# Moving the experts' first-weight loads to SyncE's queue, weighting the batch sums on VectorE, halving the maxima across engines and copying gate rows less often

## The chip, the core and the metric

The kernel runs on one core of a Trainium2 chip. The core has TensorE (PE in the profile, its weight loads PEld), VectorE (DVE), ScalarE (ACT), GpSimd (POOL) and SyncE (SP). They run on their own and wait for one another by semaphores. Work is done on tiles in SBUF (128 partitions); TensorE writes to PSUM. SP, ACT and POOL can issue transfers (DMAs). The metric is the device time in microseconds (us) of one execution: the median of three runs before the change is 1496.69 us (1496.05 to 1498.59).

## What is computed

```python
def _attn_ref(x, filt_r, filt_i):            # x 8 x 3072 x 256
    X = np.fft.rfft(x, axis=1)
    Y = X * (filt_r + 1j * filt_i)[None, :, :]
    return np.fft.irfft(Y, n=x.shape[1], axis=1)

def _moe_ref(x, phi, w1, w2):                # x 24576 x 256, 8 experts of 4 slots
    logits = x @ phi                         # 24576 x 32
    d = exp(logits - logits.max(0));  d /= d.sum(0) + 1e-9
    slot_input = d.T @ x                     # 32 x 256, over all eight batches
    for e in range(E):
        h = np.maximum(slot_input[e] @ w1[e], 0.0)
        slot_out[e] = h @ w2[e]
    c = exp(logits - logits.max(1));  c /= c.sum(1) + 1e-9
    return c @ slot_out

def _moe2_ref(x, w_gate, w_val, w_out):
    g = x @ w_gate
    return (g * sigmoid(g) * (x @ w_val)) @ w_out
```

Output: 24576 x 256, float32.

## The kernel before

The kernel has three parts, one after the other: `phase1`, `transition`, `phase2`.

**Phase 1** transforms the eight batches. A step is one half (128 columns) of a batch, 16 steps with 6 units each; the loop `for i, (s, u) in enumerate(units)` writes out by hand, unit by unit, what each engine does, and every engine works in that order. A unit multiplies by the DFT (`s2_unit`, line 258), multiplies with the filter on VectorE (lines 262 and 263, tiles P and Q), adds on POOL, and two units later transposes on TensorE (`tr_unit`, line 283, one PSUM buffer T) with an evacuation on ScalarE (line 284, tile y). Beside it run generators that the loop steps on:

- `chain(b)`, one for each batch: the logits (tile lg in SBUF, copied from PSUM by ScalarE at line 400), the maximum of each slot (VectorE, line 398, over both PSUM halves at once, then a transpose at line 411 and a second maximum at line 412 into mb), the exponentials (lines 423, 429, 434), a transform of them (lines 447 to 474), and the product with the transformed batch (line 482), which gives the batch's sum for the slots. The sums of batches 0 to 5 go out to memory and come back into `slots` (`kept`); batch 6 is copied there (line 496).
- `conv`: a rounding of w_gate, w_val and w_out on ScalarE, VectorE and POOL, in the pool `cvp` (8 KB in each partition).
- `first_weights`: the combine weights c of batch 0.

In the last two steps the experts' first weights are loaded (`load_w1`, line 134, 512 KB each): thirteen issues from ScalarE's queue, three from SyncE's after the loop (expert 6 and half of 7). Behind the loop the end of chain 6 (`g6`) and chain 7 (`g7`) are taken in turns: `for g in (g6, g7, g6, g7, g7, g6, g7, g6, g6)`. `combine` forms each batch's weight from the maxima (`al`, `beta4`), spreads it over a diagonal `rb`, and 14 small products (line 548) add seven batches' weighted sums; line 502 adds the eighth. That is `slot_input`.

**Transition**: `load_w2` (line 765, 1 MB each, from SP's queue in the order 6, 7, 0, gate weights, 5, 4, 1, 2, 3, value weights), the experts' first product (`stage1`, line 807), second product (`stage2`, line 832, first with experts 0 to 3), and with its result the small gate and value matrices for phase 2 (`g4`, `v4`). These hold in 128 rows four copies of 32: a rounded part (hi) and the rest (lo). The first third is split on VectorE (line 872); the two others are made as `gh` and `gl` (lines 886, 887) and copied by 16 DMAs (line 890), 8 from SP and 8 from POOL.

**Phase 2** runs 576 items of 512 tokens x 128 columns: gate and value products (lines 983, 984), SiLU on ScalarE (line 986, tile s), product and split on VectorE and ScalarE (h, hi, lo: lines 992, 999, 1000), and LAG items later the projection into four PSUM tiles (lines 1011 and 1015). `load_out(f)` splits the output weights wo (ScalarE line 972, POOL line 973) for items 0 to 11. Every twelfth item the four tiles are evacuated (lines 1024, 1025) and written out (line 1028).

SBUF is handed out in pools as stacks from the left and from the right. The tiles of the transition lie in a row from the left: w2_0 (8 KB), hs (8), w2_1 to w2_3 (24), ht (8), so and sot (2), gh (2), gl (2), a pad (10), and on. Phase 2's pool `kp` is opened when they have been given back, from the left again: s 3 x 2, h 3 x 2, hi 5 x 2, lo 5 x 2, tmp 4 x 1, ot 2 x 4 KB, 44 KB in all. A pool that takes over memory waits with its first instruction on each engine until everything that used that memory is done.

Of the kernel before, what the change touches and what calls it, by code (L numbers as in the profile page):

```python
# [22 lines left out]
EXP_AT = 17  # L23
HOLD = 9
# [55 lines left out]
def spectral_softmoe_glu_kernel(  # L80
# [56 lines left out]
    def phase1():  # L137
        with ExitStack() as c1:
# [4 lines left out]
            cvp = c1.enter_context(tc.tile_pool(name="cvp", bufs=1))  # L143
# [164 lines left out]
            def chain(b, last):  # L308
# [78 lines left out]
                cm = chp.tile([128, E], F32, tag="cm", name="cm")  # L387
# [9 lines left out]
                both = bass.AP(pl[0].tensor, pl[0].offset, [list(pl[0].ap[0]), [16, E], [512, 2], [1, 16]])  # L397
                dve.tensor_reduce(out=cm, in_=both, axis=AX.XY, op=ALU.max)
                for h in range(2):
                    act.copy(lg[h], pl[h].rearrange("p (e n) -> p e n", n=16))  # L400
# [11 lines left out]
                dve.tensor_reduce(  # L412
                    out=mb[:, b:b + 1],
                    in_=ps[0:32, 0:128].rearrange("p (g n) -> p g n", g=2)[:, :, 0:48],
# [30 lines left out]
                for h in range(2):  # L445
                    for g in range(2):
                        pe.matmul(
                            out=pl[64 * h:64 * h + 64, g],
                            lhsT=s1t_sb[64 * g:64 * g + 48, :],
                            rhs=dd[64 * g:64 * g + 48, h],  # L450
                            tile_position=(64 * g, 64 * h),
                        )
                for es in es2:
                    turn(bd, pl[:, :, es].rearrange("p g e n -> p e g n"), es)
                yield
                ps = two(True)
                for jj in range(NJ):
                    g, k = jj % 4, jj // 4
                    pe.matmul(
                        out=col(ps, k)[32 * g:32 * g + 32],  # L460
                        lhsT=bd[:, :, jj],
                        rhs=fwd[:, jj, :],
                        tile_position=(0, 32 * g),
                    )
                dt_ = evac("dt", ps)
# [7 lines left out]
                for k in range(6):  # L473
                    pe.transpose(out=col(ps, k), in_=col(dt_, k), identity=ident)
                if last:
                    rb, pss = next(com)
                dh = evac("dh", ps)
                yield
                ps = two(True)[0] if b == NB - 2 else small()
                for k in range(6):  # L480
                    for g in range(4):
                        pe.matmul(  # L482
                            out=ps[32 * g:32 * g + 32, 0:D],
                            lhsT=col(dh, 4 * k + g, 32),
                            rhs=yt[b, k][:, g, :],
                            start=(k == 0),
                            stop=(k == 5),
                            tile_position=(0, 32 * g),
                        )
                    if k in (2, 5) and b == NB - 2:  # L490
                        yield
# [4 lines left out]
                act.copy(sl, ps[:, 0:256])  # L496
                if b < NB - 2:
                    nc.scalar.dma_start(out=sld[:, b, :], in_=sl)
                if last:
                    next(com)  # L500
                    for d_ in range(2):
                        pe.matmul(
                            out=pss[d_][:, 0:32], lhsT=sl[:, d_ * 128:(d_ + 1) * 128], rhs=rb[:, b, :],
                            start=False, stop=True,
                        )
                        (dve.tensor_copy if d_ else act.copy)(sp[:, d_, :], pss[d_][:, 0:32])
# [10 lines left out]
            def combine():  # L517
# [5 lines left out]
                beta4 = chp.tile([128, NB, 1], F32, tag="beta4", name="beta4")  # L523
                dve.tensor_reduce(out=mx, in_=mb, axis=AX.X, op=ALU.max)
                dve.tensor_scalar(al, mb, mx, None, ALU.subtract)
                act.activation(al, al, AF.Exp)
                yield
# [4 lines left out]
                dve.tensor_scalar(al, al, sm, 2.0 / SEQ, ALU.mult, ALU.mult)  # L532
                yield
                rb = chp.tile([128, NB, 32], F32, tag="t4", name="rb")
                psb = ps_t.tile([128, 512], F32, tag="T", name="psb")
                pe.matmul(out=psb[:, 0:NB], lhsT=rep4[0:32, :], rhs=al)
                dve.tensor_copy(beta4[:, :, 0], psb[:, 0:NB])
                dve.tensor_tensor(
                    out=rb,
                    in0=rep4[:, None, 0:32].to_broadcast([128, NB, 32]),  # L540
                    in1=beta4.to_broadcast([128, NB, 32]),
                    op=ALU.mult,
                )
                pss = [ps_x.tile([128, 512], F32, tag="X", name="pss") for _ in range(2)]
                yield rb, pss
                for d_ in range(2):
                    for b in range(NB - 1):
                        pe.matmul(
                            out=pss[d_][:, 0:32],
                            lhsT=slots[b // 4][:, b % 4, d_ * 128:(d_ + 1) * 128],  # L550
                            rhs=rb[:, b, :],
                            start=(b == 0),
                            stop=False,
                        )
                yield

# [90 lines left out]
            xp += [cr.enter_context(tc.tile_pool(name=f"xp{k}", bufs=1, side="right")) for k in (1, 0)][::-1]  # L647
            load_x(0, 0)
# [52 lines left out]
            for i, (s, u) in enumerate(units):  # L701
# [16 lines left out]
                if (s, u) in ((2 * NB - 2, 0), (2 * NB - 1, 0)):  # L718
                    wt = xp[s % 2].tile([128, 2, 2, FE], F32, tag="x", name="w")
                    for k in range(2):  # L720
                        load_w1(nc.scalar, 2 * (s % 2) + k, enumerate(wt[:, k, t] for t in range(2)))
                if (s, u) == (2 * NB - 1, 0):
                    load_w1(nc.scalar, 4, [(t, sgp.tile([128, FE], F32, tag="sg", name="w")) for t in range(2)])
                if (s, u) == (2 * NB - 1, 1):
                    wt = bp[0].tile([128, 3, FE], F32, tag="b", name="w")
                    load_w1(nc.scalar, 5, ((0, wt[:, 0]), (1, wt[:, 1])))
                    load_w1(nc.scalar, 7, ((0, wt[:, 2]),))
# [10 lines left out]
            load_w1(nc.sync, 6, ((0, wt[:, 0]), (1, wt[:, 1])))  # L738
            load_w1(nc.sync, 7, ((1, wt[:, 2]),))
# [7 lines left out]
            for g in (g6, g7, g6, g7, g7, g6, g7, g6, g6):  # L747
                next(g, None)
# [7 lines left out]
    def transition():  # L756
# [13 lines left out]
        w2s[0] = one([128, 8, D], "w2_0")  # L770

# [9 lines left out]
        one([128, 10 * D], "pad")  # L781
# [82 lines left out]
        for w, dst in gates:  # L864
# [6 lines left out]
            for r in (32, 96):  # L871
                dve.tensor_tensor(out=dst[r:r + 32, :], in0=pg[r:r + 32], in1=dst[r:r + 32, :], op=ALU.subtract)
# [25 lines left out]
    def phase2_tiles():  # L898
# [7 lines left out]
        def first():  # L906
            t = cp.tile([128, 3, 2, 512], F32R, tag="c4", name="c4", bufs=2)

            for r in range(4):
                (nc.sync if r < 2 else nc.scalar).dma_start(  # L910
                    out=t[32 * r:32 * r + 32].rearrange("p q G n -> p q (G n)").bitcast(F32),
                    in_=cd[r // 2].rearrange("q e n -> e q n"),
                )
            c4[0] = t
            for c in range(3):
# [3 lines left out]
                )  # L919

        def build(b):
# [31 lines left out]
            for q in range(3):  # L953
                for r in range(4):
                    nc.sync.dma_start(
                        out=t[32 * r:32 * r + 32, q].rearrange("p G n -> p (G n)").bitcast(F32),
                        in_=(ch if r < 2 else cl)[32 * q:32 * q + 32, :].bitcast(F32),
# [4 lines left out]
        return {"cp": cp, "g4": g4, "v4": v4, "wo": wo, "c4": c4, "build": build, "first": first}  # L962

    def phase2(later):
        cp, g4, v4, wo, c4, build = (later[k] for k in ("cp", "g4", "v4", "wo", "c4", "build"))
# [3 lines left out]

        def load_out(f):  # L970
            st = wo[f][:, 1, :].bitcast(F32)
            act.copy(wo[f][:, 0, :], st)
            pool.tensor_tensor(out=wo[f][:, 1, :], in0=st, in1=wo[f][:, 0, :], op=ALU.subtract)  # L973
# [28 lines left out]

        def proj(i):
            b, q, G, f = items[i]
            hi, lo = hhi.pop(i), hlo.pop(i)
            if f == 0:
                acc[0] = [ps_o.tile([128, 512], F32, tag=f"o{t}", name=f"o{t}") for t in range(4)]
            for t in range(4):
                a = acc[0][t]
                ts = slice(128 * t, 128 * t + 128)  # L1010
                pe.matmul(  # L1011
                    out=a, lhsT=hi[:, ts], rhs=wo[f].rearrange("p k d -> p (k d)"),
                    start=(f == 0), stop=(f == NF - 1), skip_group_check=True,
                )
                pe.matmul(  # L1015
                    out=a[:, D:2 * D], lhsT=lo[:, ts], rhs=wo[f][:, 0, :],
                    start=False, stop=(f == NF - 1), skip_group_check=True,
                )
            if f == NF - 1:
                ot = kp.tile([128, 4, D], F32, tag="ot", name="ot", bufs=2)  # L1020
                for t in range(4):
                    a = acc[0][t]
                    tmp = kp.tile([128, D], F32, tag="tmp", name="tmp", bufs=4)
                    act.copy(tmp, a[:, D:2 * D])  # L1024
                    dve.tensor_tensor(out=ot[:, t, :], in0=a[:, 0:D], in1=tmp, op=ALU.add)  # L1025
# [14 lines left out]
        todo = list(range(len(items)))  # L1040
        gen = build(1)
        for i in range(len(items) + LAG):
# [11 lines left out]
            if i < NF:  # L1054
                load_out(i)
            if 0 <= i - 1 < len(items):
                split(i - 1)
            if i % 4 == 1 and i > NF:
                next(gen, None)

# [36 lines left out]
```

## Time and profile before

| | |
|---|---|
| median of three runs | 1496.69 us |
| the profiled execution: its own time, its span | 1495.89 us, 1494.1 us |
| phase 1 with its end, until the experts' first product | 0 to 379.7 us |
| transition, until the first gate product | 379.7 to 405.9 us |
| phase 2 | 405.9 to 1494.1 us |
| TensorE busy, share of the span | 96% |
| VectorE, ScalarE | 78%, 64% |

The profile is one execution. Its times count from the span's start; "idle" stands in brackets behind an instruction with what ended it. PEclk is the share of TensorE's full clock that was granted. Instructions that issue DMAs are shown on queues of their own (SPq, ACTq).

### The profile page before, as it was taken

What the parts mean: (1) busy time and instruction counts of PE and PEld (TensorE: products, weight loads), DVE (VectorE), ACT (ScalarE), POOL (GpSimd) and SP (SyncE); (2) the same over time, 40 slices, a digit from 0 to 9 for tenths busy, and PEclk for the clock granted to TensorE, in tenths of its full rate; (3) what the DMA queues carried; (4) which work ended last, traced back from release to release, by engine and by line L of the source; (5) the groups of instructions that cost most, each with busy time, mean ns of one, the idle gap of its engine ahead of it and who ended that gap; (6) DMA issues with size and microseconds to landing.
All of it is one profiled execution on the core that took longest, in us unless ns stands there. A gap on an engine that the chain in (4) does not pass through costs nothing.

```text
span 1494.1 us, 25173 instructions
## 1 busy us (share of the span) xinstructions
PE 1441.1 (96%) x9574; PEld 1152.9 (77%) x9574; DVE 1158.3 (78%) x1870; ACT 960.8 (64%) x1838; POOL 243.1 (16%) x315
## 2 busy tenths in 40 slices
PE   4899999998999999999999999999999999999998
PEld 2566566665488888888888888888888888888887
DVE  2788888876278878878887887888789778877775
ACT  1476666653267667666766766676676667666665
POOL 0466666653020000000000000000000000000000
PEclk9999999999999999999999999999999999999999
DMA  9978888859710220120031012112110211211011
GB/s 225 159 122 156 155 145 149 156 151 364 254 39 16 52 58 17 44 64 18 25 71 29 25 36 55 34 29 49 47 29 22 65 39 24 48 43 26 19 29 29
DMA packets 87848, 116.42 MB, mean 78 GB/s; under 512 B 8880, under 2 KB 65072, under 8 KB 87600
## 3 DMA queue, kind: packets, MB, share of 16 engines
q1 hardware_dynamic: 80480, 102.37, 31.4%
q10 hardware_dynamic: 6800, 11.54, 2.6%
q8 instruction: 75, 1.23, 0.4%
q0 software_dynamic: 448, 0.92, 0.2%
q14 instruction: 45, 0.37, 0.1%
HBM read 68.13 MB, written 34.60 MB: 69 GB/s over the span
## 4 chain that ended last, share of the span: by engine, by line
PE 84%; DVE 7%; DMA 3%; ACT 2%; issue 2%; POOL 1%; ACTq 0%; SPq 0%; DVEq 0%; POOLq 0%
PE o L1011 35%; PE o L1015 18%; PE V L984 9%; PE G L983 9%; PE X L258 3%; PE s L230 2%; PE T L283 2%; DVE sg L238 2%; DVE Q L263 1%; PE c L482 1%; DMA fraw<-in_filt_i_dram 1%; DVE P L262 1%; PE L L291 1%; DMA nyq<-in_filt_r_dram 1%; DMA lgf<-lgd 1%
## 5 line engine op out<-in xcount | busy, mean ns | idle before, releaser
L1011 PE MATMUL o<-wo,hi 128*128 128x512 f32 x2304 | 833.4, 396 | 2.7 <-POOL wo L973 2.7
L1015 PE MATMUL o<-wo,lo 128*128 128x256 f32 x2304 | 645.5, 280 | 0.0
L986 ACT ACTIVATE s<-G 128x512 f32<-128x512 f32 x576 | 344.7, 598 | 323.1 <-PE G L983 320.1
L992 DVE TENSOR_TENSOR h<-V,s 128x512 f32<-128x512 f32 x576 | 395.0, 686 | 172.0 <-ACT s L986 171.2
L1011 PEld LDWEIGHTS o<-wo,hi 128*128 128x128 f32 x2304 | 433.1, 188 | 106.8 <-POOL wo L973 3.0
L1015 PEld LDWEIGHTS o<-wo,lo 128*128 128x128 f32 x2304 | 434.8, 189 | 25.3
L1000 DVE TENSOR_TENSOR lo<-h,hi 128x512 fp32r<-128x512 f32 x576 | 422.4, 733 | 1.1
L999 ACT CAST hi<-h 128x512 fp32r<-128x512 f32 x576 | 354.6, 616 | 11.7 <-DVE h L992 8.3
L984 PE MATMUL V<-c,v 128*128 128x512 f32 x576 | 227.7, 395 | 1.1 <-DVE h L992 1.1
L983 PE MATMUL G<-c,g 128*128 128x512 f32 x576 | 228.3, 396 | 0.2 <-ACT s L986 0.2
L258 PEld LDWEIGHTS X<-fwd,b 128*128 128x128 f32 x768 | 94.3, 193 | 58.5 <-issue 40.0
L983 PEld LDWEIGHTS G<-c,g 128*128 128x128 f32 x576 | 108.3, 188 | 26.2 <-ACT s L986 0.9
L238 DVE STREAM_TRANSPOSE sg<-s 128x1024 f32<-128x1024 f32 x64 | 79.3, 1241 | 60.0 <-PE s L230 57.7
L258 PE MATMUL X<-fwd,b 128*128 128x128 f32 x768 | 110.6, 288 | 3.3 <-ACT b L247 1.8
L984 PEld LDWEIGHTS V<-c,v 128*128 128x128 f32 x576 | 108.8, 189 | 3.1 <-DVE h L992 2.4
L930 POOL TENSOR_TENSOR lg<-lg,mx 96x1024 f32<-96x1024 f32 x7 | 16.9, 2409 | 565.8 <-DVE mx L928 565.8
L1025 DVE TENSOR_TENSOR ot<-o,tmp 128x256 f32<-128x256 f32 x192 | 70.1, 423 | 39.6 <-ACT tmp L1024 39.6
L247 ACT COPY b<-sg 128x768 f32<-128x768 f32 x64 | 58.9, 923 | 64.6 <-DVE sg L238 64.5
L230 PE MATMUL s<-x,csm 48*64 48x512 f32 x512 | 73.4, 636 | 20.0 <-DMA x<-in_x_dram 17.5
L271 POOL TENSOR_TENSOR yt<-P 128x256 f32<-128x256 f32 x96 | 70.3, 732 | 115.9 <-DVE P L262 115.1
L262 DVE TENSOR_TENSOR P<-X,ft 128x512 f32<-128x512 f32 x96 | 64.1, 668 | 12.2 <-PE X L258 11.3
L273 POOL TENSOR_TENSOR yt<-Q 128x256 f32<-128x256 f32 x95 | 71.1, 748 | 0.2
(197 smaller groups left out, 979.9 us busy)
## 6 DMA issues: line engine op xcount, KB each, us to landing
out_dram<-ot SPq DMA_DIRECT2D x192, 128.0 KB, 2.2
x<-in_x_dram SPq DMA_DIRECT2D x60, 384.0 KB, 8.2
w<-in_moe_w_dram SPq DMA_DIRECT2D x8, 1024.0 KB, 11.4
w<-in_moe_w_dram ACTq DMA_DIRECT2D x13, 512.0 KB, 7.8
c<-ch SPq DMA_DIRECT2D x42, 128.0 KB, 2.4
c<-cl SPq DMA_DIRECT2D x42, 128.0 KB, 2.4
raw<-in_moe_w_gate_dram SPq DMA_DIRECT2D x12, 256.0 KB, 5.8
raw<-in_moe_w_val_dram SPq DMA_DIRECT2D x12, 256.0 KB, 5.2
```

Of the source, the lines that this page charges most:

```text
L230: pe.matmul(out=ps[64 * k:64 * k + 64, 16 * r:16 * r + 16, :], lhsT=s1t_sb[64 * r:64 * r + 48, :], rhs=xt[step][64 * r:64 * r + 48, k, :, ...
L238: dve.transpose(out=sg.rearrange("p j d k -> p d j k"), in_=ps.rearrange("p n d -> p d n"))
L258: pe.matmul(out=ps[:, g].rearrange("p r m -> p (r m)"), lhsT=bb[:, j, :], rhs=fwd[:, j, :])
L262: dve.tensor_tensor(out=P, in0=ps, in1=f, op=ALU.mult)
L983: pe.matmul(out=pg, lhsT=g4[c][:, fs], rhs=c4[b][:, q, G, :])
L984: pe.matmul(out=pv, lhsT=v4[c][:, fs], rhs=c4[b][:, q, G, :])
L986: act.activation(s, pg, AF.Silu)
L992: dve.tensor_tensor(out=h, in0=pv, in1=s, op=ALU.mult)
L999: act.copy(hi, h)
L1000: dve.tensor_tensor(out=lo, in0=h, in1=hi, op=ALU.subtract)
L1011: pe.matmul(out=a, lhsT=hi[:, ts], rhs=wo[f].rearrange("p k d -> p (k d)"), start=(f == 0), stop=(f == NF - 1), skip_group_check=True,)
L1015: pe.matmul(out=a[:, D:2 * D], lhsT=lo[:, ts], rhs=wo[f][:, 0, :], start=False, stop=(f == NF - 1), skip_group_check=True,)
```

## The change

- The maxima: VectorE takes the maximum of one PSUM half while ScalarE's copy is written for the other, and then the other way round; the two columns of maxima are transposed by two products.
- The batch sums: `combine` adds the weighted sums on VectorE in seven steps (`add`), placed between steps of chain 7, and the eighth as the evacuation of the product; the 14 products of line 548 go. Chain 6's last product is cut into four pieces, and the pieces stand between the steps of chain 7.
- The loads: all first weights go out from SP's queue. `cvp` is on the right now, is given back at the last step's first unit, and expert 6's weights take its place. w2_0 leaves the left end of the row and stands behind gl; it is loaded last but one.
- The gates: rows are ordered hi, hi, lo, lo, so that one subtraction does for two; three `load_out` steps (EARLY) are moved ahead of the copies. Of the 16 copies 12 are issued by SP and 4 by POOL.
- The last two items are projected tile by tile (`part`, `evac`, `close`), and each pair of tiles is written out when it is done, from three queues.

```diff
+EARLY = 3
...
-            cvp = c1.enter_context(tc.tile_pool(name="cvp", bufs=1))
+            cvs = ExitStack()
...
+                plv = [t.rearrange("p (e n) -> p e n", n=16) for t in pl]
                 for h in range(2):
-                    act.copy(lg[h], pl[h].rearrange("p (e n) -> p e n", n=16))
+                    dve.tensor_reduce(out=cm[:, h], in_=plv[1 - h], axis=AX.X, op=ALU.max)
+                    act.copy(lg[h], plv[h])
...
-                pe.transpose(out=ps[0:32, 0:128], in_=cm, identity=ident)
+                for h in range(2):
+                    pe.transpose(out=ps[0:32, 128 * h:128 * h + 128], in_=cm[:, h], identity=ident)
...
-                    if k in (2, 5) and b == NB - 2:
+                    if k >= 2 and b == NB - 2:
                         yield
...
-                act.copy(sl, ps[:, 0:256])
+                if last:
+                    rb, beta4, acc = next(com)
+                    dve.scalar_tensor_tensor(sl, ps[:, 0:256], beta4[:, b:b + 1], acc, ALU.mult, ALU.add)
+                else:
+                    act.copy(sl, ps[:, 0:256])
...
+                def add(b):
+                    row = slots[b // 4][:, b % 4, :]
+                    if b == 0:
+                        dve.tensor_scalar(row, row, beta4[:, 0:1], None, ALU.mult)
+                    else:
+                        acc = slots[0][:, 0, :]
+                        dve.scalar_tensor_tensor(acc, row, beta4[:, b:b + 1], acc, ALU.mult, ALU.add)
+
+                for b in range(3):
+                    add(b)
                 yield
...
-                for d_ in range(2):
-                    for b in range(NB - 1):
-                        pe.matmul(
...
+            cvp = cvs.enter_context(tc.tile_pool(name="cvp", bufs=1, side="right"))
...
-                        load_w1(nc.scalar, 2 * (s % 2) + k, enumerate(wt[:, k, t] for t in range(2)))
+                        load_w1(nc.sync, 2 * (s % 2) + k, enumerate(wt[:, k, t] for t in range(2)))
...
+                if (s, u) == (2 * NB - 1, 0):
+                    for _ in side:
+                        pass
+                    cvs.close()
+                    w6 = cr.enter_context(tc.tile_pool(name="w6", bufs=1, side="right"))
+                    load_w1(nc.sync, 6, enumerate(w6.tile([128, FE], F32, tag=f"w{t}", name="w") for t in range(2)))
...
-            for g in (g6, g7, g6, g7, g7, g6, g7, g6, g6):
+            for g in (g6, g7, g6, g7, g7, g6, g7, g6, g7, g6, g7, g6, g6):
...
-        w2s[0] = one([128, 8, D], "w2_0")
...
-        one([128, 10 * D], "pad")
+        w2s[0] = one([128, 8, D], "w2_0")
+        one([128, 2 * D], "pad")
...
-        for e in (6, 7, 0):
+        for e in (6, 7):
             load_w2(e)
         flat_load(wg, wd[0], 128)
-        for e in (5, 4, 1, 2, 3):
+        for e in (5, 4, 1, 2, 3, 0):
             load_w2(e)
...
-            for r in (32, 96):
-                dve.tensor_tensor(out=dst[r:r + 32, :], in0=pg[r:r + 32], in1=dst[r:r + 32, :], op=ALU.subtract)
+            dve.tensor_tensor(out=dst[64:128, :], in0=pg[64:128], in1=dst[64:128, :], op=ALU.subtract)
+
+        for f in range(EARLY):
+            later["load_out"](f)
...
-                (nc.sync if r < 2 else nc.gpsimd).dma_start(
+                (nc.sync if r % 2 or c == 2 else nc.gpsimd).dma_start(
                     out=later[n][c][32 * r:32 * r + 32, :].bitcast(F32),
-                    in_=(gl if r % 2 else gh)[32 * i:32 * i + 32, :].bitcast(F32),
+                    in_=(gl if r >= 2 else gh)[32 * i:32 * i + 32, :].bitcast(F32),
...
+        def close(two):
+            b, q, G, _ = items[two[0]]
+            ot = kp.tile([128, 4, D], F32, tag="ot", name="ot", bufs=2)
+            row = b * SEQ + 1024 * q + 16 * G
+            for t in range(4):
+                for i in two:
+                    part(i, t)
+                evac(ot, t)
+                if t % 2:
+                    for ii in range(4):
+                        (nc.sync if ii % 2 == 0 else nc.scalar if t == 3 else nc.gpsimd).dma_start(
+                            out=bass.AP(out.tensor, (row + 4 * ii + t - 1) * D, [[32 * D, 32], [1, 2 * D]]),
+                            in_=ot[32 * ii:32 * ii + 32, t - 1:t + 1].rearrange("p t d -> p (t d)"),
+                        )
```

`part(i, t)` is one tile's two products of the old `proj`, `evac` its evacuation; neither is new work.

How the built programs stand at three places follows. Line numbers are each program's own; a name in the brackets is a counter that the row waits for. SP's transfers use eight counters, DMAHW0 to DMAHW7, in turn, and a transfer waits for the one before it on its counter.

The maxima of chain 7 on VectorE (cm the maxima of the slots, cl the PSUM tile with both halves of the logits), before:

```order
L467 TENSOR_SCALAR dt<-dt 32x1 [waits Activation_49]
L398 TENSOR_REDUCE cm<-cl 128x32 [waits PE_49]
L412 TENSOR_REDUCE mb<-c 32x1 [waits PE_49]
L423 TENSOR_TENSOR dd<-lg,c 128x512 [waits PE_49,Activation_49]
L423 TENSOR_TENSOR dd<-lg,c 128x512 [waits Activation_49]
```

and now, with ScalarE's rows of the same place (lg the copied logits) behind it:

```order
L473 TENSOR_SCALAR dt<-dt 32x1 [waits Activation_49]
L400 TENSOR_REDUCE cm<-cl 128x32 [waits PE_49]
L400 TENSOR_REDUCE cm<-cl 128x32 [waits Activation_49]
L414 TENSOR_REDUCE mb<-c 32x1 [waits PE_49]
L425 TENSOR_TENSOR dd<-lg,c 128x512 [waits PE_49]
L425 TENSOR_TENSOR dd<-lg,c 128x512 [waits Activation_49]
```

```order
L337 COPY dt<-cl 128x512 [waits PE_49,Pool_49]
L341 COPY dt<-cl 128x256 [waits PE_49]
L474 COPY sb__63<-dt 32x1 [waits DVE_49]
L401 COPY lg<-cl 128x512 [waits DVE_49,Pool_49] x2
L337 COPY dh<-cl 128x512 [waits PE_49]
```

One maximum has become two; the second waits for ScalarE's copy, and each of the two copies waits for VectorE, where before only the first did. The seven chains before stand the same way.

The experts' second weights on SP, before:

```order
L765 DMA w2_6_4739<-in_moe_w2_dram 128x2x1024 [waits DMAHW3_49,DVE_49]
L765 DMA w2_7_4743<-in_moe_w2_dram 128x2x1024 [waits DMAHW4_49]
L765 DMA w2_0_4671<-in_moe_w2_dram 128x2x1024 [waits DMAHW7_49,DMAHW5_49]
L127 DMA wg_4755<-wgd_66 128x2x1536 [waits DMAHW6_49,PE_49]
L765 DMA w2_5_4735<-in_moe_w2_dram 128x2x1024 [waits DVE_49,PE_49,DMAHW7_49,Activation_49,Pool_49]
```

and now, from expert 5 on:

```order
L782 DMA w2_5_4752<-in_moe_w2_dram 128x2x1024 [waits DVE_49,PE_49,DMAHW6_49,Activation_49,Pool_49]
L782 DMA w2_4_4748<-in_moe_w2_dram 128x2x1024 [waits DMASW2_49,DMASW3_49,DMASW1_49,DMAHW7_49,DMASW0_49,DVE_49]
L782 DMA w2_1_4696<-in_moe_w2_dram 128x2x1024 [waits DMAHW0_49]
L782 DMA w2_2_4700<-in_moe_w2_dram 128x2x1024 [waits DMAHW1_49]
L782 DMA w2_3_4704<-in_moe_w2_dram 128x2x1024 [waits DMAHW3_49]
L782 DMA w2_0_4740<-in_moe_w2_dram 128x2x1024 [waits DMAHW4_49,PE_49]
L128 DMA wv_4776<-wvd_67 128x2x1536 [waits DMAHW6_49]
```

w2_0 has moved from ahead of the gate weights to the last place but one. In both programs the wait for PE of expert 5's load is that for the last piece of chain 6's product, and what follows on SP stands behind it.

ScalarE where phase 2 starts (s the first SiLU results, gh the rounded gate rows), before:

```order
L870 CAST v4_0_4830<-h_4938 128x512 [waits PE_49]
L886 CAST gh_4719<-t_4944 128x512 [waits PE_49]
L986 ACTIVATE s_5011<-G_5007 128x512 [waits DMAHW2_49,DMAHW3_49,DMAHW1_49,PE_49]
L972 CAST wo0_4833<-wo0_4833 128x256 [waits DMAHW1_49]
L986 ACTIVATE s_5021<-G_5017 128x512 [waits PE_49]
```

and now, with SP's copies behind it (the last of the twelve that SP issues is left out):

```order
L886 CAST v4_0_4848<-h_4955 128x512 [waits PE_49]
L941 CAST wo0_4851<-wo0_4851 128x256 [waits DMAHW1_49]
L941 CAST wo0_4851<-wo0_4851 128x256 x2
L904 CAST gh_4732<-t_4966 128x512 [waits PE_49]
L1004 ACTIVATE s_5033<-G_5029 128x512 [waits DMAHW1_49,DMAHW3_49,DMAHW0_49,DMAHW4_49,DMASW6_49,DMAHW5_49,DMASW4_49,DMAHW6_49,DVE_49,PE_49]
```

```order
L908 DMA g4_1_4846<-gh_4732 32x512 [waits DMAHW4_49,Activation_49]
L908 DMA g4_1_4846<-gl_4736 32x512 [waits DMAHW5_49,DVE_49]
L908 DMA v4_1_4849<-gh_4732 32x512 [waits DMAHW6_49]
L908 DMA v4_1_4849<-gl_4736 32x512 [waits DMAHW7_49]
L908 DMA g4_2_4847<-gh_4732 32x512 [waits DMAHW0_49]
L908 DMA g4_2_4847<-gh_4732 32x512 [waits DMAHW1_49]
L908 DMA g4_2_4847<-gl_4736 32x512 [waits DMAHW2_49]
L908 DMA g4_2_4847<-gl_4736 32x512 [waits DMAHW3_49]
L908 DMA v4_2_4850<-gh_4732 32x512 [waits DMAHW4_49]
L908 DMA v4_2_4850<-gh_4732 32x512 [waits DMAHW5_49]
L908 DMA v4_2_4850<-gl_4736 32x512 [waits DMAHW6_49]
```

The first SiLU waited for three earlier weight loads; now it waits for the counters of all copies out of gh, of which the last, on DMAHW5, is the tenth that SP issues.

## Rows read from the trace of the kernel before

**Rows 1.** Page: busy time, share of the span and instructions of each engine

```profile
PE 1441.1 (96%) x9574; PEld 1152.9 (77%) x9574; DVE 1158.3 (78%) x1870; ACT 960.8 (64%) x1838; POOL 243.1 (16%) x315
```

**Rows 2.** Table of windows: PE, PEld, DVE, ACT, POOL busy, PEclk, DMA share, GB/s

```profile
45.00:315.00 270.00, 257.52 (x2771) 169.33 (x2768) 227.53 (x352) 174.96 (x362) 168.41 (x233) 1.00 0.85 151
360.00:363.20 3.20, 1.71 (x13) 1.02 (x9) 1.97 (x3) 1.60 (x4) 0.72 (x2) 1.00 1.03 407
363.20:366.70 3.50, 3.49 (x30) 1.33 (x32) 2.45 (x6) 1.65 (x4) 2.05 (x4) 0.53 1.03 417
375.00:387.00 12.00, 11.35 (x90) 6.16 (x83) 1.08 (x3) 1.26 (x4) 0.00 (x0) 0.86 1.02 409
406.00:411.80 5.80, 2.88 (x8) 1.25 (x8) 5.15 (x9) 5.31 (x12) 4.64 (x10) 0.95 0.60 133
411.80:418.00 6.20, 6.13 (x18) 5.16 (x19) 4.12 (x3) 1.41 (x3) 2.80 (x5) 0.50 0.44 111
```

**Rows 3.** Waits of TensorE, 45 to 315 us: total, times, longest

```profile
PE T L283 <- ACT y L284: 3.7, 5, 0.9
```

**Rows 4.** Timeline, 171 to 176 us: start, duration, engine, line; a loop chain

```profile
171.28 1.21 DVE L398 TENSOR_REDUCE cm<-c 128x32 f32<-128x1024 f32 x1
172.41 0.67 DVE L262 TENSOR_TENSOR P<-X,ft 128x512 f32<-128x512 f32 x1
172.52 1.07 ACT L400 COPY lg<-c 128x512 f32<-128x512 f32 x2 [1.02 <-DVE cm L398]
174.23 0.63 PE L283 MATMUL T<-csm,yt 128*128 128x128 f32 x4 [0.93 <-ACT y L284]
```

**Rows 5.** Timeline, 344 to 347 us: end of the loop

```profile
344.22 1.37 ACTq L134 DMA_DIRECT2D w<-in_moe_w_dram  x2
346.36 0.63 PE L283 MATMUL T<-csm,yt 128*128 128x128 f32 x4 [0.49 <-ACT y L284]
```

**Rows 6.** Timeline, 367 to 392 us: chains 6 and 7, then the experts

```profile
367.29 1.50 PE L482 MATMUL cl<-y,dh 128*32 128x256 f32 x24
368.98 3.83 SPq L765 DMA_DIRECT2D w<-in_moe_w_dram  x5
372.58 1.93 PE L482 MATMUL c<-y,dha 128*32 128x256 f32 x32
375.31 3.31 PE L548 MATMUL pss<-rb,slots 128*128 128x32 f32 x28
379.72 7.05 PE L807 MATMUL h<-w,stm 128*32 128x512 f32 x48 [0.65 <-PE pss L502]
389.92 1.93 PE L832 MATMUL o<-w,ht 128*32 128x256 f32 x32
```

**Rows 7.** DMA issues, 372.6 to 374 us: KB each, us to landing

```profile
w<-in_moe_w_dram SPq DMA_DIRECT2D x1, 1024.0 KB, 14.4
```

**Rows 8.** Timeline, 406 to 412 us: phase 2 starts

```profile
406.05 0.59 ACT L886 CAST gh<-t 128x512 fp32r<-128x512 f32 x1 [1.30 <-PE t L878]
406.53 0.60 ACT L986 ACTIVATE s<-G 128x512 f32<-128x512 f32 x1
406.66 0.61 SPq L890 DMA_DIRECT2D g<-gh  x1
407.39 0.52 SPq L890 DMA_DIRECT2D g<-gl  x1
408.71 0.50 PE L984 MATMUL V<-c,v 128*128 128x512 f32 x1
410.55 0.59 SPq L890 DMA_DIRECT2D v<-gh  x1
411.87 0.80 PE L1011 MATMUL o<-wo,hi 128*128 128x512 f32 x1 [2.67 <-POOL wo L973]
```

**Rows 9.** DMA issues, 400 to 412 us: the copies out of gh

```profile
g<-gh SPq DMA_DIRECT2D x2, 64.0 KB, 3.0
```

**Rows 10.** Timeline, 1489 to 1492 us: the last writes

```profile
1489.67 1.72 SPq L1028 DMA_DIRECT2D out_dram<-ot  x4
```

More of the change, by code (lines that the diff above doesn't have):

```diff
@@ L464, in chain @@
                     )
+                if last:
+                    next(com)
                 dt_ = evac("dt", ps)
@@ L499, in chain @@
                 if last:
-                    next(com)
                     for d_ in range(2):
-                        pe.matmul(
[L503 to L506, printed above, removed]
+                        pss = ps_x.tile([128, 512], F32, tag="X", name="pss")
+                        pe.matmul(out=pss[:, 0:32], lhsT=sl[:, d_ * 128:(d_ + 1) * 128], rhs=rb)
+                        (dve.tensor_copy if d_ else act.copy)(sp[:, d_, :], pss[:, 0:32])
                 for u in range(6):
@@ L531, in combine @@
                 dve.reciprocal(sm, sm)
[L532 removed]
                 yield
[L534 to L545, printed above, removed]
[L546 to L554 removed]
+                psn = ps_l.tile([128, 512], F32, tag="L", name="psn")
+                pe.matmul(out=psn[:, 0:1], lhsT=rep4[0:32, :], rhs=sm)
+                rb = chp.tile([128, 32], F32, tag="t4", name="rb")
+                nrm = chp.tile([128, 1], F32, tag="nrm", name="nrm")
+                dve.tensor_copy(nrm, psn[:, 0:1])
+                dve.tensor_scalar(rb, rep4[:, 0:32], nrm, 2.0 / SEQ, ALU.mult, ALU.mult)
+                for b in range(3, NB - 2):
+                    add(b)
                 yield
+                add(NB - 2)
+                yield rb, beta4, slots[0][:, 0, :]
             def flat(a):
@@ L919, in first, with load_out @@
                 )
+        def load_out(f):
+            st = wo[f][:, 1, :].bitcast(F32)
+            act.copy(wo[f][:, 0, :], st)
+            pool.tensor_tensor(out=wo[f][:, 1, :], in0=st, in1=wo[f][:, 0, :], op=ALU.subtract)
         def build(b):
@@ L1001, in split, with part, evac @@
             hhi[i], hlo[i] = hi, lo
+        def part(i, t):
+            f = items[i][3]
+            a = acc[0][t]
+            ts = slice(128 * t, 128 * t + 128)
+            pe.matmul(
+                out=a, lhsT=hhi[i][:, ts], rhs=wo[f].rearrange("p k d -> p (k d)"),
+                start=(f == 0), stop=(f == NF - 1), skip_group_check=True,
+            )
+            pe.matmul(
+                out=a[:, D:2 * D], lhsT=hlo[i][:, ts], rhs=wo[f][:, 0, :],
+                start=False, stop=(f == NF - 1), skip_group_check=True,
+            )
+        def evac(ot, t):
+            a = acc[0][t]
+            tmp = kp.tile([128, D], F32, tag="tmp", name="tmp", bufs=4)
+            act.copy(tmp, a[:, D:2 * D])
+            dve.tensor_tensor(out=ot[:, t, :], in0=a[:, 0:D], in1=tmp, op=ALU.add)
+        def close(two):
[11 more added lines that the diff above has]
+                            in_=ot[32 * ii:32 * ii + 32, t - 1:t + 1].rearrange("p t d -> p (t d)"),
+                        )
         def proj(i):
             b, q, G, f = items[i]
-            hi, lo = hhi.pop(i), hlo.pop(i)
             if f == 0:
@@ L1008, in proj @@
             for t in range(4):
[L1009 to L1018, printed above, removed]
+                part(i, t)
+            hhi.pop(i)
+            hlo.pop(i)
             if f == NF - 1:
@@ L1021, in proj @@
                 for t in range(4):
[L1022 to L1025, printed above, removed]
+                    evac(ot, t)
                 row = b * SEQ + 1024 * q + 16 * G
@@ L1038, in lag @@
             return min(LAG, 3 + i // 10)
-        todo = list(range(len(items)))
+        todo = list(range(len(items) - 2))
         gen = build(1)
```

45 lines of the change are left out of this document (23 added, 22 removed).

## Prediction

> **What bounds the kernel now.** I read the page first: TensorE is busy for 96% of the span [rows 1], so a saving counts only where TensorE waits or where its own work goes. The table of windows shows where that is. In the loop of phase 1 it works 257.52 of 270 us [rows 2], and the waits list names the little that can be had there: five waits of the transposes for ScalarE's y, 3.7 us in all [rows 3]. The timeline of a loop chain shows how that wait arises: VectorE's maximum, 1.21 us, then ScalarE's two copies, and the y that the next transpose needs stands behind them; TensorE is idle 0.93 us [rows 4]. The end of chain 7, the experts and the start of phase 2 are a chain of short steps with waits between them; their rows are in the timeline [rows 6, 8]. The windows add the clock: after the sparse 360 to 363.2 us, TensorE 1.71 of 3.20 us busy, the granted clock is 0.53 for 3.5 us, and after the sparse 406 to 411.8, 2.88 of 5.80, it is 0.50 for 6.2 us [rows 2], which is the 1.2 GHz level in place of 2.4. So a pause of TensorE has cost more here than its own length.
>
> The sum is made against the profiled execution, 1495.9 us (span 1494.1 and 1.8 around it); the median of the runs, 1496.7, lies 0.8 above it. A measurement of this kernel can tell 0.2%, 3 us, from no change.
>
> **1. The maxima.** In the order of the changed program the four reads of a chain's logits form one line: the first copy waits for the first maximum, the second maximum for that copy, the second copy for that maximum. So the halves are read in turn, not side by side. A VectorE operation on 128x512 from PSUM takes 0.67 us [rows 4], a copy of that size 0.60 (as the SiLU [rows 8]). Four in line are 0.67 + 0.60 + 0.67 + 0.60 = 2.54, with 0.1 for the hand-overs 2.65; before, from the maximum's start to the copies' end it was 171.28 to 173.59, 2.31 [rows 4]. ScalarE's next y is 0.35 later, TensorE already waits for it, and the second transpose adds about 0.1 (a product of this size is between 0.06, 24 in 1.50 [rows 6], and 0.16, four in 0.63 [rows 4]). 0.45 in each of seven loop chains is **+3.2 us**. The ends: 0, if the waits swallow it, and +9.0, if also VectorE's longer hold (0.67 + 0.60 + 0.67 + 0.1 = 2.05 in place of 1.21, +0.84 a chain) passes through P to TensorE. I exclude a gain, since the reads stand in one line. I take 3.2, nearest to the one wait that the trace shows.
>
> The Trainium skill, PSUM — Partial Sum Buffer, section "PSUM bank collisions raise a hardware error", says that ScalarE and VectorE may read PSUM at the same time as long as they are in different banks; by that rule the crossed halves would overlap, and this term would be about -3 in place of +3.2. No run here shows it, and the order above waits all the same.
>
> **2. First weights from SP.** The thirteen issues cost ScalarE's queue 0.68 us each (two in 1.37), and one wait of TensorE behind them shows, 0.49 us [rows 5]. It goes: -0.5 (0 to -0.9). On SP the issues stand where it has few others, and the rounding whose home expert 6 takes is over before the last step. Expert 6 comes earlier, which nobody waits for. This term is in the 372.4 below.
>
> **3. Batch sums, chain 6 in pieces, w2_0 last.** The products of line 548, 3.31 us [rows 6], leave the path. The seven steps on VectorE lie beside chain 7; only the last one follows its product, some 0.4 us, estimated from the 0.67 for twice its size. TensorE alone would come to the experts' second product at 389.92 - 3.31 + 0.4 - 0.5 + 0.35 = 386.9. But what is queued behind the second weights decides. Expert 5's load waited for the end of chain 6's product: that ended at 368.79, the load went out at 368.98 [rows 6]. The last piece of that product now stands just ahead of chain 7's, which began at 372.58; with -0.5 and +0.35 that is 372.4, the load 0.2 later. Six loads of 1 MB stand behind that wait, and the one that the second product needs first, w2_0, is the sixth. At the 409 GB/s of that stretch [rows 2] 6.29 MB take 15.4 us, with 2.2 to land w2_0 is there at 390.2. The other end comes from the loads before: five issued from 368.98, the last landed at 372.6 + 14.4 = 387.0 [rows 6, 7], 18.0 after the first; one more at 2.6 makes 20.6, thus 393.2. I take 391.3, nearer to the first, since the gate weights that were still moving at 369 are through by then. The second product starts at 391.3 in place of 389.92: **+1.4** (+0.3 to +3.3), the saving of 3.3 is gone, and TensorE pauses for 4.4 us.
>
> **4. The clock after it.** The half-speed stretches behind pauses are 3.5 and 6.2 us long [rows 2]; half of each is lost: 1.75 to 3.1. I take **+1.8** (0 to 3.1), since TensorE is dense ahead of this pause.
>
> **5. The start of phase 2.** The early output weights remove the 2.67 us for which the first projection waited for POOL [rows 8]; the three casts on ScalarE fit into the 1.30 us ahead of gh, or nearly. But the 8 KB of w2_0 have left the front of the row, so gh now begins at 42 KB, and phase 2's pool of 44 KB lies over it. In the order the first SiLU therefore waits for all copies out of gh. The tenth of SP's twelve copies is the last of them. SP issued its first at 406.66, the second 0.73 later, then one each 0.63 (407.39 to 410.55 in five [rows 8]): the tenth goes out at 406.66 + 0.73 + 8 x 0.63 = 412.4 and lands 3.0 later [rows 9], 415.4 in place of a SiLU at 406.53. From that SiLU to the fourth gate pair's end, where the first projection could have started, it took 409.21 - 406.53 = 2.7 [rows 8]: the first projection starts at 418.1, not 411.87, +6.2. Some of the half-speed stretch now falls in that restart, where TensorE waits anyway: -1.0, so **+5.1** rounded (ends +3.0, all of the 3.1 given back, and +6.8, with slow gates ahead). The queue behind: SP's own last copies end by 417, ahead of their use in items 4 and 8.
>
> **6. The end.** Four writes stood in line on SP, 1.72 us, 0.43 each [rows 10]. For the last pair there are two on SP and two on ScalarE, and the earlier pair is out already: **-0.9** (0 to -1.3). The gate subtractions come in front of the SiLU's wait and cost or give nothing.
>
> Sum: 3.2 + 1.4 + 1.8 + 5.1 - 0.9 = +10.6. 1495.9 + 10.6 = 1506.5; as a median, 0.8 more, **1507**.
>
> **Rivals.**
> - Not slower: the first SiLU does not hold. It decides from the moment the tenth copy lands later than the first gate product ends, 406.5. If the copies land ahead of that, or the wait is not there, term 5 becomes a gain: -2.7 of POOL's wait, and -3.1 of the slow clock behind it, in place of +5.1. That gives 1507.3 - 10.9 = 1496.4. For it speaks only that in the trace before the SiLU waited for no copy [rows 8]; against it speak the waits in the order. 0.07.
> - w2_0 lands in time. If SP's queue is empty so early that six loads go faster, or chain 6's last piece ends by 368, the second product starts at 386.9: -3.0 in place of +1.4, and term 4 goes: 1501.1. Against it speaks the 409 GB/s with a DMA share of 1.02 [rows 2], already full. 0.10.
> - The halves do overlap, as the change says. Then maximum and copies take about 1.4 in place of 2.31, ScalarE's y comes earlier than TensorE wants it, and most of the 0.6 to 0.9 goes, less the second transpose: -3.0 in place of +3.2, 1501.1. 0.03.
> - VectorE's hold passes on: +9.0 in place of +3.2, 1513. Against it speaks that in the loop TensorE waits for ScalarE far more than for POOL or VectorE. 0.10.
> - The forecast has the rest, 0.70.
>
> **How the numbers follow.** The forecast's own range is 1502 to 1511: the terms' ends (3.2 down, 3.1 up and so on) seldom meet. The range goes down to the second and third rival with the lower terms, 1499, and up to the fourth, 1513; that leaves out the first rival and the fringes. Faster by over 0.2%: the better half of the first rival, and the second with the maxima free as well, 0.05. Within 0.2%: the rest of the first, and the second with its lower ends, 0.10. Slower: 0.85.
>
> **What would show it.** Right: the first SiLU is idle for some 8 to 9 us behind gh, ended by a copy out of gh, and the first projection starts 11 to 12 us after gh's rounding (5.8 before); the experts' second product waits 3 to 5 us for w2_0's load and a granted clock near 0.5 follows; ScalarE's copies of the logits stand idle between VectorE's two maxima, and the transposes wait 1.0 to 1.3 us once in each loop chain. Wrong: a first projection within 5 us of gh, or a second product that follows the first without a wait, or maxima and copies that overlap. A gain in phase 2's steady part would be one that I see no reason for.

## The result and the profile after

Six runs of the changed kernel have a median of 1512.32 us (1507.58 to 1515.25), six of the kernel before 1495.58. The ratio is 1.0111, with a 95% interval of 1.0098 to 1.0124: by it, **16.6 us slower**. The forecast was 1507, the range 1499 to 1513. The profiled execution is the slowest of the six, 1515.25 us (span 1513.5); its mean granted clock is 0.985, that of the other five 0.987 to 0.993.

The two profiles differ by 19.4 us of span. Cut at the events that the prediction speaks of (cm of chain 7 is its first maximum), the stretches are:

| stretch | before | after | difference |
|---|---|---|---|
| start to cm of chain 7 | 360.28 | 367.99 | +7.7 |
| to the experts' first product | 19.44 | 17.29 | -2.2 |
| to their second product | 10.20 | 19.26 | +9.1 |
| to gh's rounding | 16.13 | 18.00 | +1.9 |
| to the first projection | 5.82 | 11.40 | +5.6 |
| to the end | 1082.23 | 1079.56 | -2.7 |

First the loop. The waits list of TensorE, 45 to 325 us of the changed kernel, answers to [rows 3] (which reads the same up to 325 us):

```profile
PE T L284 <- ACT y L285: 7.2, 6, 1.8
```

3.7 us have become 7.2. The timeline of chain 4 shows how, as [rows 4] did for a chain before:

```profile
257.45 0.68 DVE L400 TENSOR_REDUCE cm<-c 128x32 f32<-128x512 f32 x1
258.16 0.58 ACT L401 COPY lg<-c 128x512 f32<-128x512 f32 x1 [1.07 <-DVE cm L400]
258.78 0.69 DVE L400 TENSOR_REDUCE cm<-c 128x32 f32<-128x512 f32 x1 [0.65 <-ACT lg L401]
259.50 0.58 ACT L401 COPY lg<-c 128x512 f32<-128x512 f32 x1 [0.76 <-DVE cm L400]
260.72 0.63 PE L284 MATMUL T<-csm,yt 128*128 128x128 f32 x4 [1.84 <-ACT y L285]
```

The four reads stand in line, from 257.45 to 260.08, 2.63 us. TensorE's pause is 1.84 us, and the table of windows (columns as in [rows 2]) shows what follows it:

```profile
256.00:260.00 4.00, 2.76 (x24) 2.30 (x20) 3.35 (x7) 2.17 (x6) 2.87 (x4) 1.00 0.00 0
260.00:264.00 4.00, 3.28 (x22) 1.01 (x22) 2.80 (x7) 2.35 (x7) 3.71 (x6) 0.74 0.80 246
264.00:268.00 4.00, 4.00 (x22) 3.31 (x22) 2.72 (x4) 1.62 (x3) 1.33 (x3) 0.50 0.96 209
268.00:272.00 4.00, 4.00 (x19) 2.39 (x15) 2.55 (x4) 2.96 (x6) 0.66 (x1) 0.50 1.11 266
```

Half clock for some 10 us; the loop is 3.5 us later than before at VectorE's transpose ahead of it (254.19 for 250.66) and 7.9 behind it (277.85 for 269.99). No such stretch stands in the loop of the kernel before between 36 and 360 us. Of the 3.5, 1.3 is there at the first chain's maximum already (89.77 for 88.49); the granted clock falls now and then in the first 72 us of either kind of kernel, and that maximum starts between 88.0 and 90.3 in the seven profiles with one maximum over both halves, so this 1.3 is scatter.

Next the experts. The timeline, answering to [rows 6]:

```profile
381.02 3.19 SPq L782 DMA_DIRECT2D w<-in_moe_w_dram  x6
385.28 5.36 PE L823 MATMUL h<-w,stm 128*32 128x512 f32 x48 [0.61 <-DVE stm L815]
393.24 0.84 ACTq L928 DMA_DIRECT2D c<-cd  x2
404.54 3.64 PE L848 MATMUL o<-w,ht 128*32 128x256 f32 x32 [10.69 <-DMA w<-in_moe_w_dram]
```

The six loads go out 13.0 us behind cm of chain 7 (before: 8.7), and TensorE stands still for 10.69 us until w2_0 is there, 23.5 us after the first of the six. The sixth issue, w2_0's, stands at 383.8; the two loads on ACTq are half of those of the combine weights c of batch 0, 384 KB each. The windows behind that pause:

```profile
400.00:404.00 4.00, 0.00 (x0) 0.00 (x0) 0.00 (x0) 0.00 (x0) 0.00 (x0) 0.50 1.03 280
404.00:408.00 4.00, 3.46 (x32) 1.58 (x32) 0.00 (x0) 0.00 (x0) 0.00 (x0) 0.50 1.04 330
```

The first 32 products take 3.64 us, 1.93 before [rows 6]. Last the start of phase 2, the answer to [rows 8]:

```profile
422.54 0.59 ACT L904 CAST gh<-t 128x512 fp32r<-128x512 f32 x1 [0.39 <-PE t L896]
423.15 0.61 SPq L908 DMA_DIRECT2D g<-gh  x1
...
428.29 1.22 SPq L908 DMA_DIRECT2D v<-gh  x2
...
431.12 0.60 ACT L1004 ACTIVATE s<-G 128x512 f32<-128x512 f32 x1 [7.99 <-DMA v<-gh]
...
433.94 0.64 PE L1025 MATMUL o<-wo,hi 128*128 128x512 f32 x1
```

The first SiLU holds 7.99 us for the last copy out of gh. The first projection waits for POOL no longer, and starts 11.40 us after gh.

### The profile page after: what moved, and what is told of

It reads as the page before. It is cut to its first block, busy times and chain, and to the rows that moved or that the text cites. A ratio compares the mean times of both kernels' runs of the same rounds, so it can differ in the third digit from the quotient of the medians.

```text
span 1513.5 us, 25161 instructions
## 1 busy us (share of the span) xinstructions
PE 1444.1 (95%) x9556; PEld 1154.3 (76%) x9556; DVE 1161.2 (77%) x1884; ACT 961.1 (64%) x1837; POOL 242.7 (16%) x313
## 4 chain that ended last, share of the span: by engine, by line
PE 84%; DVE 8%; DMA 3%; ACT 2%; issue 2%; SPq 1%; POOL 0%; DVEq 0%; ACTq 0%; POOLq 0%
PE o L1025 35%; PE o L1029 18%; PE V L1002 9%; PE G L1001 9%; PE X L259 4%; PE s L231 3%; DVE sg L239 2%; PE T L284 2%; DMA w<-in_moe_w_dram 1%; DVE Q L264 1%; DVE P L263 1%; DMA x<-in_x_dram 1%; PE L L292 1%; PE c L488 1%; DMA lgf<-lgd 1%
## 5 line engine op out<-in xcount | busy, mean ns | idle before, releaser
L259 PE MATMUL X<-fwd,b 128*128 128x128 f32 x768 | 113.7, 293 | 2.3 <-ACT b L248 1.2
```

The lines of the kernel that those rows point to most:

```text
L259: pe.matmul(out=ps[:, g].rearrange("p r m -> p (r m)"), lhsT=bb[:, j, :], rhs=fwd[:, j, :])
```

## The experiments

Each ratio is to runs of the kernel before on the same chip (medians 1494.2 to 1495.1), with its 95% interval.

**gh out of phase 2's memory** (the changed kernel):

```diff
+        w2s[0] = one([128, 8, D], "w2_0")
         gh = one([128, 512], "gh", dt=F32R)
         gl = one([128, 512], "gl", dt=F32R)
-        w2s[0] = one([128, 8, D], "w2_0")
```

> The changed kernel with w2_0 placed ahead of gh and gl, so that gh lies at 50 KB again, beyond phase 2's pool of 44 KB; all else as changed. Theory (the first SiLU holds for the copies out of gh, 7.99 us idle in the changed kernel's trace): the SiLU follows the gate product within 1 us of gh's rounding, the first projection comes about 3 us after gh (11.4 in the changed kernel), and the time falls by 7 to 9 us, to about 1504. Rival (SP's longer line of copies or the second pair of gates would hold phase 2 anyway): the SiLU's wait goes to another transfer and the time falls by under 3 us.

Measured: 1.0067 (1.0052 to 1.0083), 1505.1 us. The timeline of its phase 2:

```profile
416.33 0.59 ACT L904 CAST gh<-t 128x512 fp32r<-128x512 f32 x1 [0.39 <-PE t L896]
416.82 0.60 ACT L1004 ACTIVATE s<-G 128x512 f32<-128x512 f32 x1
...
419.33 0.40 PE L1025 MATMUL o<-wo,hi 128*128 128x512 f32 x1
```

The hold is gone: 3.00 us from gh to the first projection, not 11.40. Of those 8.4 us the ratio shows 1.0111 - 1.0067 = 0.44%, 6.6 us. The two intervals leave some 3 us either way, so the runs do not show that the rest is missing.

**One maximum over both halves** (the changed kernel):

```diff
...
+                dve.tensor_reduce(out=cm, in_=both, axis=AX.XY, op=ALU.max)
                 for h in range(2):
-                    dve.tensor_reduce(out=cm[:, h], in_=plv[1 - h], axis=AX.X, op=ALU.max)
-                    act.copy(lg[h], plv[h])
+                    act.copy(lg[h], pl[h].rearrange("p (e n) -> p e n", n=16))
...
```

> The changed kernel with one maximum over both halves, as before, and one transpose of it. Theory (four reads in line, +0.45 a chain, and in the profiled run a fall of the clock to 0.50 for some 8 us behind a 1.84 us wait of the transpose): the seven waits of the transposes for y are back under 1 us, no stretch at half clock in the loop between 72 and 350 us, and the time falls by 3 us, or by 6 to 7 where the changed kernel has the fall: a median of 1506 to 1509 and runs closer together than the changed kernel's 7.7 us. Rival (the loop's loss is from the loads and the moved pool): the loop stays as long, less than 1 us gained.

Measured: 1.0096 (1.0080 to 1.0113), 1508.4 us, four runs from 1507.4 to 1509.0. Against 1.0111 that is 2.2 us less, which the intervals do not tell from nothing; the trace and the next run show the effect. The waits of the transposes are back at 3.7 us, no half clock between 72 and 350, and cm of chain 7 is at 360.34 (before 360.28).

**Halved maxima alone** (the kernel before with this part of the change, the diff above the other way round):

> The kernel before with one part of the change alone: the maxima by halves and their two transposes. Theory (four reads of PSUM in line in each chain): the wait of the transposes for ScalarE's y behind a chain grows by about 0.4 us, seven times, so 3 us slower than before (1497 where before is 1494), and 4 us more in a run where such a wait is followed by half clock in the loop. Rival (the loop's waits swallow it): within 1 us of before.

Measured: 1.0029 (1.0017 to 1.0041), 4.3 us slower, 12 runs from 1495.7 to 1503.5. TensorE's waits list reads as in the changed kernel:

```profile
PE T L283 <- ACT y L284: 7.2, 6, 1.8
```

Its profile has the half clock from 261.6 to 271.6 us as well. Of the five profiles with halved maxima three have a fall of the clock there, of the seven with one maximum none has between 72 and 350 us. The two without it (gh out of phase 2's memory, and chain 6's pieces together, the next run) have the same wait, 1.85 us, so the wait alone does not decide. From the first chain's first maximum to chain 7's it is 270.7 to 272.2 us in the seven, 274.1 in those two, 274.5 in the third with a fall, which lasts only 3 us there (c's loads from one queue, below), and 278.2 in the changed kernel and 278.0 here: some 2.6 us for the waits and 4 for the fall.

**Chain 6's pieces together** (the changed kernel):

```diff
-            for g in (g6, g7, g6, g7, g7, g6, g7, g6, g7, g6, g7, g6, g6):
+            for g in (g6, g7, g6, g7, g7, g6, g7, g6, g6, g6, g6, g7, g7):
```

> The changed kernel with the four pieces of chain 6's last product next to one another, ahead of chain 7's last steps, not in turns with them. Theory (the six loads wait for the last piece, and the experts' second product for w2_0, the sixth: 10.69 us idle): the load of expert 5 goes out 4 to 5 us earlier, the second product starts 4 to 9 us earlier, total 1504 to 1508. Rival (w2_0 is late because the combine weights' and output weights' loads share the DMA engines from 393 us on): the second product gains under 2 us.

Measured: 1.0052 (1.0034 to 1.0070), 1501.0 us, some 9 us less than the changed kernel, and more of a gain than expected. The loads go out 11.2 us behind cm of chain 7, not 13.0, and w2_0 is there 19.1 us after the first, not 23.5:

```profile
374.18 6.77 SPq L782 DMA_DIRECT2D w<-in_moe_w_dram  x6
...
393.31 1.93 PE L848 MATMUL o<-w,ht 128*32 128x256 f32 x32 [2.26 <-DMA w<-in_moe_w_dram]
```

Counted from cm of chain 7, w2_0 is there 6.3 us sooner. The earlier issue explains 1.8 of that, not the 4.4 by which the six are quicker. Behind the shorter pause, 2.26 us, the 32 products take 1.93 us, not 3.64. So the rival has a share, and the next run asks for it.

**c's loads from one queue** (the changed kernel):

```diff
-                (nc.sync if r < 2 else nc.scalar).dma_start(
+                nc.sync.dma_start(
```

> The changed kernel with the four loads of the combine weights c all from SP's queue, where they stand behind w2_0 and the value weights; in the changed kernel two of them go out from ScalarE's queue at 393 us, while w2_0 is still on its way. Theory (they take a share of the DMA engines from w2_0, which lands 23.5 us after the first of the six loads went out, but 19.1 after it in the run in which the six go out earlier): w2_0's load lands about 19 to 20 us after the first of the six, the experts' second product waits 6 to 7 us and not 10.7, total about 4 us less, 1507. Rival (the transfers are limited by their own bytes and packets): the wait stays above 9.5 us.

Measured: 1.0071 (1.0054 to 1.0087), 1505.6 us.

```profile
377.93 3.14 SPq L782 DMA_DIRECT2D w<-in_moe_w_dram  x6
...
396.99 3.64 PE L848 MATMUL o<-w,ht 128*32 128x256 f32 x32 [6.23 <-DMA w<-in_moe_w_dram]
```

The wait is 6.23 in place of 10.69, and w2_0 lands 19.1 us after the first load. Two loads of 384 KB from a queue that is not SP's cost w2_0 4.4 us; the two other runs above that leave these loads and chain 6's pieces as changed have 23.2 and 23.7. The traces also show how. In the changed kernel all queues together move 408 GB/s from 395 to 397 us, at a DMA share of 1.02, and 271 GB/s from 397 to 403, at 1.05; ScalarE's queue has 48% of the engines' time in those 6 us, and SP's moves 0.90 MB. With all four loads of c on SP's queue the rate from 400 to 406 us, behind w2_0, is 206 GB/s at a share of 1.04. So c's bytes move at about half the rate of the weights: 0.79 MB at 206 GB/s are, as an estimate, 3.8 us of the 4.4. Why they are slow no run shows.

**Early splits alone** (the kernel before; `load_out` for items 0 to 2 ahead of gh's rounding):

```diff
...
+        for f in range(EARLY):
+            later["load_out"](f)
...
```

> The kernel before with one part of the change alone: three splits of the output weights moved ahead of the rounding of gh. Theory (POOL's 2.67 us is what the first projection waits for, and half clock behind it): the first projection starts about 3 us after gh instead of 5.8, the half-speed stretch of 6.2 us gets shorter or goes: 2.7 to 5.8 us faster than before, 1490 to 1493. Rival (what is late next is VectorE's first lo, or the casts delay gh): under 1 us gained.

Measured: 0.9989 (0.9979 to 0.9998), 0.3 to 3.1 us faster. From gh to the first projection it is 2.99 us, not 5.82, and no window behind it is at half clock; but from there to the end the profile is only 0.5 us shorter than before, with waits of 0.66 for a copy and 0.91 for VectorE's lo where the half clock was. The clock's part of the expectation failed.

**Batch sums alone** (the kernel before with the change's `combine`; all loads and chain 6 as before):

> The kernel before with the batch sums added on VectorE, the order of chain 6 and of all loads left as before. Theory (the 14 products of line 548 are 3.31 us of the path, and without them the experts start earlier; w2_0 to w2_3 have landed by 387.0): the time from chain 7's maxima to the experts' first product falls from 19.4 by 2.5 to 3.3 us, the second product follows without a wait for a load, total 2.5 to 3.3 us faster than before. Rival (the loads bound the second product at once): the second product waits for a load and the gain is under 1 us.

Measured: 0.9972 (0.9961 to 0.9982), 1490.7 us, 4.2 us faster, a little above what was expected. From cm of chain 7 to the experts' first product it is 17.17 us, not 19.44, and the second follows at 384.64 without a wait.

**Sums, early splits and the closed end** (the kernel before with these three):

> The kernel before with three parts of the change: batch sums on VectorE (as in the run above), three early splits of the output weights, and the last two items closed tile by tile. Theory: the parts add up: 2.5 to 3.3 from the sums, 0.7 to 2.7 from the early splits, 0.8 to 1.3 from the end: 4 to 7 us faster than before, 1487 to 1490 where before is 1494. Rival (what one part gains, a load or a fall of the clock takes back): under 3 us faster.

Measured: 0.9957 (0.9944 to 0.9969), 1488.0 us, **6.4 us faster than before**.

**Four edits undone** (the changed kernel):

> The changed kernel with the four edits of the runs above together: gh behind w2_0, one maximum over both halves, chain 6's pieces next to one another, c's loads from SP's queue. Theory (these places hold nearly all that the change lost): no SiLU hold, no fall of the clock in the loop, 2 us or less of wait for w2_0: 1491 to 1495, no slower than before, since the sums, the early splits and the end give about 6 and w2_0 and chain 6 ahead of chain 7 take some back. Rival (a loss that the runs above did not name, in the moved pool or SP's queue): still over 1498.

Measured: 0.9958 (0.9945 to 0.9971), 1489.0 us: faster than before, by a little more than expected. No SiLU hold, no half clock between 72 and 360 us, 2.64 us of wait for w2_0. Together the four edits give 22.9 us. The kernel is as fast as the one with the three gaining parts alone (0.9957), so these four places held what the change lost, within the 3 us that the two intervals leave; its other parts gain or lose nothing that these runs show.

**First weights from SP's queue** (the kernel with the three parts):

```diff
-                        load_w1(nc.scalar, 2 * (s % 2) + k, enumerate(wt[:, k, t] for t in range(2)))
+                        load_w1(nc.sync, 2 * (s % 2) + k, enumerate(wt[:, k, t] for t in range(2)))
...
```

The three other calls that went out from ScalarE's queue are changed the same way.

> The kernel with sums on VectorE, early splits and the closed end (the fastest so far, 1488) with all first weights from SP's queue, their memory as before. Theory (an issue costs ScalarE's queue 0.68 us and one wait of TensorE of 0.49 us shows behind them): 0.3 to 0.9 us faster than that kernel, 1487 to 1488. Rival (nothing waits there, or SP's queue delays the second weights): equal within 1 us or slower.

Measured: 0.9948 (0.9935 to 0.9962), 1487.6 us, the fastest here. Beside the 0.9957 of the kernel without it the intervals overlap: whether the queue gives the 0.5 us or nothing stays open.

## Why the prediction was right, and where not

The direction and the three mechanisms were right: the maxima in line, the wait for w2_0, the SiLU's hold. 1512.3 lies in the range, but that owes something to luck: the forecast's own range ended at 1511, and the 1513 came from the fourth rival, which did not happen. The profiled execution is 19.4 us longer than before, where the sum has 10.6. Term by term, from the table:

- **Maxima, +3.2.** The waits of the transposes grew by 7.2 - 3.7 = 3.5, and the loop by 2.6 where the clock did not fall; alone the part costs 0.29%, 4.3 us. What the term left out is the clock: I had put the falls only behind the two sparse stretches of the transition, and in the loop a wait of 1.84 us was followed by one in three of five profiles, some 4 us in the changed kernel's. The order decided, as argued: the halves were not read side by side. That they would be from two banks, as the Trainium skill, PSUM — Partial Sum Buffer, section "PSUM bank collisions raise a hardware error", lets one expect, no run here shows; both halves lie in one tile, and it wasn't tried with two.
- **Sums and w2_0, +1.4.** From cm of chain 7 to the second product it is 36.55 us, 29.64 before: +6.9. This is the term that was mis-sized most. The sums took 2.2 off the path to the first product, where 3.3 - 0.4 = 2.9 was worked out. That the load behind chain 6 decides was right, and the issue was 13.0 us behind cm, at most 0.7 later than worked out (372.6 - 360.3 = 12.3). The transfer was taken as 18.7 us (372.6 to 391.3); it took 23.5. With c on SP's queue it is 19.1, so the sum of bytes and landing was good, and what I left out was the neighbour: c's loads on ScalarE's queue, which go out when the experts' last first product has ended and the first weights' memory is free (393.24). In the kernel before they go out at 389.37, but the five loads had landed by 387.0.
- **Clock after the pause, +1.8.** From the second product to gh: +1.9.
- **Start of phase 2, +5.1.** First projection against gh +5.6 (forecast +6.2). The tenth copy went out 5.8 us behind the first, as worked out, and landed 2.2 later, not 3.0. To the end -2.7 together with the closed end; from the last product's end to the span's end it is 5.3 before (1488.77 to 1494.1) and 4.6 now, -0.8. That leaves -1.9 for the slow stretch, where I took -1.0: half clock lasts some 2 us behind the first projection, 6.2 before. The term comes to +3.7. Undone, it gave 6.6, give or take 3, so the two do not contradict each other.
- **End, -0.9.** -0.8.

Of the rivals none came about as such. The fourth had the number, 1513, for another reason: VectorE's hold did not pass on to TensorE through P, ScalarE's y did it alone.

The chance of 0.85 for slower rested on waits that stand in the built order, which left little open; the sizes of what waits behind a load were the weak part.

## What to carry to other kernels

When a buffer is moved, look at what takes over its old neighbours' place: 8 KB gone from the front of a row put a tile under a pool that starts while its copies are still on their way. When a load becomes the one that is needed first, count every queue that will be busy until it lands, not its own alone, and at the rate at which that queue's bytes have been seen to move. And two engines that read "crossed" halves of one tile may be put in line by the program; the waits in the built order tell it ahead of a run.

## What was not expected of the hardware

- In all five profiles with halved maxima TensorE pauses 1.84 or 1.85 us behind chain 4's maxima, in a loop that is otherwise dense. In three of them the granted clock is 0.50 soon behind it, for some 10 us in two and 3 us in the third; in the other two it stays at 1.00. With waits of at most 1.5 us there, none of seven has a fall.
- The runs of one and the same kernel scatter with their mean clock: halved maxima alone, 1495.7 at 0.995 and 1503.5 at 0.988. The kernel before, beside them, does so too: 1490.7 at 0.997 and 1497.6 at 0.993. So the scatter is not from the halved maxima alone.
- With the DMA engines full (a share of 1.03), 0.8 MB from a second queue delayed a load that had been queued 9 us earlier by 4.4 us, more than the 1.9 us that 0.8 MB take at the 409 GB/s of [rows 2]. The share stays full while these bytes move at about half that rate: a full share does not tell how many bytes move.
